# A fused attention and two-expert-layer kernel: the sign step of the weights' conversion as a parametric relu on ScalarE, the low-part subtractions on VectorE

## The chip, the cores and the metric

The kernel runs on one core of a Trainium2 chip. The metric is the time of the whole program in device microseconds (us), lower is better. The core's engines work side by side, each through its own queue in order: TensorE (PE, matmuls), VectorE (DVE), ScalarE (ACT), GpSimd (POOL) and SyncE (SP, which issues the transfers).

## The reference

The reference chains three layers over 2304 tokens (4 batches of 576):

```python
attn = masked_softmax(q @ k.T / 8) @ v        # 8 heads: 4 with a local mask, 4 with a strided one
x = attn as (2304, 512)
h = x @ w_in                                  # 512 -> 2048
g = np.maximum(h, 0.0) ** 2
x = g @ w_out                                 # 2048 -> 512
# soft mixture of experts: 8 experts of 4 slots each
d = softmax(x @ phi, over tokens);  slots = d.T @ x
slot_out = relu(slots[e] @ w1[e]) @ w2[e]
out = softmax(x @ phi, over slots) @ slot_out
```

`w_in` and `w_out` arrive as float64 (the inputs' scaling makes them so), and the kernel is handed their raw 64-bit patterns as pairs of 32-bit words.

## The kernel before, in words

**Stages.** The tokens go in six blocks of 384. In the first stage ("the head") the attention of the first batch and part of the second is computed, the weights of the middle layer are converted, and the first block's products of that layer start as soon as their weights are there. From then on the products of blocks 1 to 5 follow, with the rest of the attention and the dispatch of the soft mixture between them; at the end come the experts and the combination.

**Products.** For each of 16 chunks `f` of the 2048 hidden columns, `gemm1` makes `h` from 12 matmuls (line 409 of the listing, weights in a high and a low part times the tokens `xr` in a high and a low part), `square` on ScalarE makes `r` (line 416) and its square's high part `gh` (419) and the full square (421), `square_low` the low part `gl` (425, VectorE or GpSimd by the letters in `LOW`), and `product` adds three groups of matmuls into `acc_ps` (434 with `gh`, 431 with `gl`).

**Conversion.** The weights go by 16 pairs of chunks `m`, each chunk a 128 x 512 tile that is loaded as 128 x 1024 words (`raw`). Four generators make one pair:

- `split1` (ScalarE): the high words, read as float32 and scaled by 2^-112, into `y` (line 362).
- `split2`: the sign step. Where `MIN[m]` is D, one `scalar_tensor_tensor` on VectorE over the pair, 128 x 1024 (line 376: times 2^32, then the smaller of that and `y`, so that negative values get another scale). Where it is P (pairs 0 and 13), two more relus on ScalarE (370) and two additions on GpSimd (373). Then, on VectorE, a shift of the bits by 3 (line 378, 128 x 1024) and, for each chunk, a merge with the low word's top bits (382, 128 x 512).
- `split3` (ScalarE): the cast of `y` to the high part of `w` (line 389).
- `split4` (GpSimd): the low part of `w`, `y` minus the high part (line 396, 128 x 512).

`y` alternates between two tiles, so pair `m + 2` may only be written when the low part of pair `m` is made.

**What sets the order.** The head's order is a string, `HEAD`: each word is a step (W for `split1` then `split2`, X for `split3`, Y for `split4`, S, C, E, T, V for the attention, R, L, g, H, O for the products, l, q, v for loads), and each word advances its generator to the next `yield`. A word for a generator that has ended does nothing:

```python
                next(parts[step], None)
```

So each engine's queue holds the head's instructions in the order of the string. From the second block on the orders of PE and SP are written out, and the others are placed by priority.

Of the kernel before, what the change touches and what calls it, by code (L numbers as in the profile page):

```python
# [33 lines left out]
LOW = 'DPDPPDDDPPPDDDPP'  # L34
MIN = 'PDDDDDDDDDDDDPDD'
WARM = 6
# [23 lines left out]
def body(tc, qd, kd, vl, vs, win, wout, phi, w1, w2, cst, out):  # L60
# [3 lines left out]
    with ExitStack() as base, ExitStack() as order:  # L64
# [20 lines left out]

# [1 line left out]
        c = cp.tile([128, C_END], F32, name="c")  # L87
# [13 lines left out]

# [1 line left out]
        class Buf:  # L103
            """Queries, keys (block-diagonal over the two heads, 32 zeros ahead), values; scores and weights."""

# [54 lines left out]
        def heads(k, a, n):  # L160
            """Columns a.. a+n of both heads' keys."""
            v = k[:, a:a + n]
            return bass.AP(v.tensor, v.offset, [v.ap[0], (S, 2), (1, n)])

        class Unit:
            """One batch and head pair: queries x keys, softmax, transposed, times values."""

            def __init__(self, b, p, u, qk_tags=("at", "at"), engines="PP", part="AB"):
                """A local unit may come in two parts: of an odd batch, A has the tokens of the first block that it is in."""
                self.b, self.p, self.u, self.part = b, p, u, part  # L170
                self.local = p < 2
                if self.local:
                    self.th = slice(0 if "A" in part else 2, 10 if "B" in part else 4)
                self.view = u.sl[:, self.th] if self.local else u.ss
                n = self.view.shape[1]
                self.mx = tiny[:, 1 if self.local else 3, 0:n]
                self.su = tiny[:, 0 if self.local else 2, 0:n]
                self.qk_tags = qk_tags
                self.ce, self.ne = (DVE if e == "D" else POOL for e in engines)
                self.nm = f"{b}_{p}"  # L180
# [67 lines left out]
            def transpose_pe(self, engines, tags=None):  # L248
                """The same through the tensor engine; each copy out by the engine that its letter names (D in `moves_dve`)."""
                o = wide.rearrange("p a b -> p (a b)")  # L250
# [38 lines left out]
            def values(self):  # L289
                p, u = self.p, self.u  # L290
                # the batch's tokens by the ring's thirds: third, its column, first token, tokens
                segs = [(1, T // 2, 0, T // 2), (2, 0, T // 2, T)] if self.b % 2 else [(0, 0, 0, T), (1, 0, T, T // 2)]
# [42 lines left out]

# [1 line left out]
        # A float64's high word read as a float32 has its exponent in steps of 8; times 2^-112  # L337
        # the exponent field becomes float32's own (2^-80 for negatives: the sign moves to the
        # bit that the shift by 3 takes to the top). The low word gives the last 3 bits.
        # The chunks go by order of first use, two at a time, each to its slot of the weights' space;  # L340
        # slots not yet filled hold the incoming bits and the values on their way.
        NW = 2 * NF
# [11 lines left out]
        def split1(m):  # L354
            if m == NF - 1:
                y = ys[m] = bt[:, 4:6]
            else:
                if m < 2:
                    ys["tile", m] = slot(NW - 2 + m, [128, 2, 512], F32, f"y{m}")
                y = ys[m] = ys["tile", m % 2]  # L360
            for z in range(2):
                ACT.activation(y[:, z], raws[2 * m + z][:, :, 1].bitcast(F32), AF.Relu if MIN[m] == "P" else AF.Copy, scale=2.0 ** -112)  # L362
                yield

        def split2(m):
            y = ys[m]
            if MIN[m] == "P":
                hi = [raws[2 * m + z][:, :, 1].bitcast(F32) for z in range(2)]
                for h in hi:
                    ACT.activation(h, h, AF.Relu, scale=-2.0 ** -80)  # L370
                    yield
                for z in range(2):
                    POOL.tensor_tensor(out=y[:, z], in0=hi[z], in1=y[:, z], op=ALU.add)
                    yield
            else:
                DVE.scalar_tensor_tensor(out=y, in0=y, scalar=2.0 ** 32, in1=y, op0=ALU.mult, op1=ALU.min)  # L376
                yield
            DVE.tensor_scalar(y.bitcast(U32), y.bitcast(U32), 3, None, op0=ALU.logical_shift_left)  # L378
            for z in range(2):
                yield  # L380
                yb = y[:, z].bitcast(U32)
                DVE.scalar_tensor_tensor(out=yb, in0=raws[2 * m + z][:, :, 0], scalar=29, in1=yb,  # L382
                                         op0=ALU.logical_shift_right, op1=ALU.bitwise_or)
# [8 lines left out]
        def split4(m):  # L392
            for z in range(2):
                kind, f = W_ORDER[2 * m + z]
                w = (w_in, w_out)[kind][f]
                POOL.tensor_tensor(out=w[:, 1], in0=ys[m][:, z], in1=w[:, 0].bitcast(F32), op=ALU.subtract)  # L396
                yield

# [1 line left out]
        hs, rs, gh, gl = {}, {}, {}, {}  # L400
# [39 lines left out]

# [1 line left out]
        m_run, s_run = st[:, 0:1], st[:, 1:2]  # L442
# [8 lines left out]
        class Dispatch:  # L451
# [17 lines left out]
            def soft(self):  # L469
# [4 lines left out]
                if self.last:  # L474
                    # one maximum for the three groups of tokens
                    for j in range(3):
                        DVE.tensor_tensor(out=st[0:32, 8 + j:9 + j], in0=st[q(j), 2:3], in1=st[q(j), 0:1], op=ALU.max)
                    DVE.tensor_reduce(out=st[0:32, 11:12], in_=st[0:32, 8:11], op=ALU.max, axis=AX.X)
                    for j in range(3):
                        DVE.tensor_scalar_mul(st[q(j), 3:4], st[0:32, 11:12], -1.0)  # L480
                else:
                    DVE.tensor_tensor(out=bm, in0=bm, in1=m, op=ALU.max)
                    DVE.tensor_scalar_mul(nm, bm, -1.0)
# [37 lines left out]

# [1 line left out]
        # In the order of use; a tile goes to the next space that falls free.  # L523
        e_order = [(k, g, j, z) for k in range(2) for g in range(2) for z in range(4) for j in range(4)]
# [19 lines left out]
        def load_e_ring(n):  # L544
            """Three tiles in the ring's n-th third, after its last use."""
            t = ringp.tile([128, 6, 512], F32, tag=f"ring{n}", bufs=1, name=f"ring{n}_{e_next[0]}")
            for y in range(3):
                load_e(lambda name: t[:, 2 * y:2 * y + 2])
# [3 lines left out]

# [1 line left out]
        order.enter_context(tc.manual_schedule())  # L554
# [4 lines left out]
        def keep_warm(n=1, a=ident, b=c[:, 0:256]):  # L559
            """Products that nothing reads: the array's clock falls when it stands still."""  # L560
            for _ in range(n):
# [61 lines left out]

# [1 line left out]
        bg = {}  # L625
# [16 lines left out]
        def last_products(g):  # L642
            """The last two slots', two of the three token groups ahead of the third."""
            for j in range(2):
# [48 lines left out]

# [1 line left out]
        d = Dispatch(NBLK - 1, last=True)  # L695
# [32 lines left out]

# [1 line left out]
        # Transposed, an expert's four slots go to four copies k = 0..3, so that group j's 32 rows of the  # L730
        # second product are (k, group of experts, slot): two copies become the high part, two the low.
        hsb = [bt[:, n] for n in range(2)]
# [4 lines left out]
        def refill(z):  # L737
            """Tiles of the first group's w1, read by now, take what is still to come."""
            for n in range(4 * z, 4 * z + 4):
# [22 lines left out]
        def turn(g, n):  # L762
            ht = acc_ps[2] if n else ps("mo", f"ht{g}")
            for z in range(4):
                # w2's rows lie in pairs, an even and an odd one in each partition
                h_ = hsb[n][:, 256 * (z // 2):256 * (z // 2) + 256].rearrange("p (x a) -> p a x", a=2)[:, z % 2, :]
# [15 lines left out]

# [1 line left out]
        spare = [freed[4 + n] for n in range(16)]  # L784
# [108 lines left out]
```

## Time and profile before

| | |
|---|---|
| three runs | 583.48, 583.71, 584.54 us; median 583.71 us |
| profiled execution, first to last instruction (span) | 583.3 us; no time beside its span is recorded for it |
| PE busy over the span | 547.7 us (94%) |
| VectorE, ScalarE, GpSimd busy over the span | 269.6, 249.7, 103.2 us |
| the same in the stretch from 48 to 121 us: PE, VectorE, ScalarE, GpSimd | 58.47, 69.29, 43.88, 51.10 us of 73 |

Busy time is what an engine spent in its own instructions; a busy share over the whole span averages stages with different limits, so the stretches are read apart. The head ends at about 142 us, when the last pair of weights is converted; 441 of the 583 us lie behind it. The runs lie within 0.2% of each other, so the comparison below calls a change of less than 0.2% no change.

### The profile page before, as it was taken

Reading aid. Unit: us, or ns where it says so; the run is one execution under the profiler, and the core shown is the slowest. Engines: PE = TensorE matmul, PEld = TensorE weight load, DVE = VectorE, ACT = ScalarE, POOL = GpSimd, SP = SyncE. Lnnn points to the kernel's source line nnn. Section 1 sums busy time; section 2 is a strip of 40 time slices with the busy share of each in tenths; the row PEclk is TensorE's granted clock in tenths of the full one; section 3 lists DMA queues with packets and bytes.
Section 4 is the critical chain, followed back from the end, with each engine's and each line's share of the span. In section 5 each row is a group of like instructions: output and inputs, shape, how many; then the busy total and the mean of one; then the engine's idle time right before and its main releaser. Section 6 shows DMA issues by size and latency. Waiting matters only on the chain.

```text
span 583.3 us, 10033 instructions
## 1 busy us (share of the span) xinstructions
PE 547.7 (94%) x4092; PEld 454.4 (78%) x4092; DVE 269.6 (46%) x565; ACT 249.7 (43%) x541; POOL 103.2 (18%) x95
## 2 busy tenths in 40 slices
PE   7878887889999999999999999999999999999994
PEld 5657666767988988888888888898889988984442
DVE  6998999954154316566135574211211113122322
ACT  2476655657443334443344343343433543341232
POOL 4528566734011001010001010000000000001000
PEclk8889999879999999999999999999999999999998
DMA  9976431330010101210221210340002566669946
GB/s 295 345 273 218 176 112 55 117 107 24 0 42 22 44 22 42 78 44 22 78 64 42 69 34 36 128 198 0 1 1 77 191 230 224 240 231 328 402 168 220
DMA packets 27117, 72.87 MB, mean 125 GB/s; under 512 B 3008, under 2 KB 8640, under 8 KB 27072
## 3 DMA queue, kind: packets, MB, share of 16 engines
q1 hardware_dynamic: 27072, 72.24, 35.2%
q8 instruction: 32, 0.52, 0.4%
q14 instruction: 13, 0.11, 0.1%
HBM read 67.51 MB, written 4.72 MB: 124 GB/s over the span
## 4 chain that ended last, share of the span: by engine, by line
PE 77%; DVE 15%; ACT 3%; issue 2%; DMA 1%; POOL 1%; SPq 0%; ACTq 0%; POOLq 0%
PE h L409 30%; PE acc_ps L434 21%; PE acc_ps L431 10%; DVE y L382 3%; PE acc_ps L779 3%; PE eh L755 2%; DVE y L376 2%; DVE y L378 2%; PE oa L311 1%; PE ob L311 1%; PE x2t L458 1%; PE lg L466 1%; DVE ptl L245 1%; DMA bt<-kd 1%; PE qa L191 1%
## 5 line engine op out<-in xcount | busy, mean ns | idle before, releaser
L409 PE MATMUL h<-xr,w 128*128 128x384 f32 x1152 | 224.7, 342 | 4.2 <-ACT r L416 3.0
L409 PEld LDWEIGHTS h<-xr,w 128*128 128x128 f32 x1152 | 207.3, 191 | 15.0 <-ACT r L416 4.8
L434 PE MATMUL acc_ps<-w,gh 128*128 128x512 f32 x576 | 155.1, 403 | 1.1 <-POOL w L396 1.1
L416 ACT ACTIVATE r<-h 128x384 f32<-128x384 f32 x96 | 47.1, 491 | 200.2 <-PE h L409 196.9
L425 DVE TENSOR_TENSOR gl<-r,gh 128x384 fp32r<-128x384 f32 x88 | 53.5, 608 | 169.6 <-ACT r L421 165.6
L434 PEld LDWEIGHTS acc_ps<-w,gh 128*128 128x128 f32 x576 | 104.3, 189 | 26.6 <-ACT gh L419 2.7
L431 PE MATMUL acc_ps<-w,gl 128*128 128x512 f32 x288 | 82.7, 394 | 4.4 <-DVE gl L425 4.4
L431 PEld LDWEIGHTS acc_ps<-w,gl 128*128 128x128 f32 x288 | 53.5, 188 | 17.7 <-DVE gl L425 6.3
L396 POOL TENSOR_TENSOR w<-y,w 128x512 fp32r<-128x512 f32 x30 | 46.0, 1543 | 34.6 <-ACT w L389 33.2
L419 ACT ACTIVATE gh<-r 128x384 fp32r<-128x384 f32 x96 | 50.0, 524 | 2.6
L421 ACT ACTIVATE r<-r 128x384 f32<-128x384 f32 x96 | 50.2, 525 | 2.0
L217 POOL TENSOR_TENSOR sl<-sl,tiny 128x640 f32<-128x640 f32 (+2 forms) x10 | 12.2, 1219 | 144.1 <-DVE tiny L214 144.1
L245 DVE STREAM_TRANSPOSE ptl<-sl 32x320 f32<-32x320 f32 (+2 forms) x72 | 31.3, 435 | 6.8 <-POOL sl L232 5.3
L735 POOL MEMSET bt<- 128x512 f32 x4 | 2.0, 525 | 175.8 <-PE lg L466 172.5
L389 ACT CAST w<-y 128x512 fp32r<-128x512 f32 x30 | 18.4, 618 | 18.4 <-DVE y L382 18.3
L382 DVE SCALAR_TENSOR_TENSOR y<-raw,y 128x512 uint32<-128x512 uint32 x26 | 25.2, 977 | 0.3
L362 ACT ACTIVATE y<-raw 128x512 f32<-128x512 f32 x26 | 17.3, 677 | 10.3 <-DMA raw<-win 10.3
L562 PE MATMUL warm<-el 128*128 128x256 f32 x54 | 19.0, 514 | 1.1 <-POOL el L555 1.1
L376 DVE SCALAR_TENSOR_TENSOR y<-y 128x1024 f32<-128x1024 f32 x13 | 19.3, 1488 | 0.8 <-ACT y L362 0.8
L562 PEld LDWEIGHTS warm<-el 128*128 128x128 f32 x54 | 13.6, 265 | 4.1 <-POOL el L555 1.1
L200 DVE SCALAR_TENSOR_TENSOR sl<-qa,c 128x128 f32<-128x128 f32 (+3 forms) x18 | 6.3, 375 | 20.7 <-PE qa L191 15.7
L245 DVE STREAM_TRANSPOSE pts<-sw 32x512 f32<-32x512 f32 x20 | 14.1, 703 | 3.7 <-POOL sw L232 3.4
(173 smaller groups left out, 481.1 us busy)
## 6 DMA issues: line engine op xcount, KB each, us to landing
e<-w SPq DMA_DIRECT2D x49, 512.0 KB, 4.6
ring<-w SPq DMA_DIRECT2D x15, 512.0 KB, 9.1
raw<-win SPq DMA_DIRECT2D x14, 512.0 KB, 6.2
raw<-wout SPq DMA_DIRECT2D x12, 512.0 KB, 8.4
out<-ob SPq DMA_DIRECT2D x18, 256.0 KB, 2.8
q<-qd SPq DMA_DIRECT2D x15, 288.0 KB, 3.6
k<-kd SPq DMA_DIRECT2D x30, 144.0 KB, 3.7
v<-vs SPq DMA_DIRECT2D x7, 512.0 KB, 4.2
```

Of the source, the lines that this page charges most:

```text
L245: DVE.transpose(out=dst, in_=src)
L376: DVE.scalar_tensor_tensor(out=y, in0=y, scalar=2.0 ** 32, in1=y, op0=ALU.mult, op1=ALU.min)
L382: DVE.scalar_tensor_tensor(out=yb, in0=raws[2 * m + z][:, :, 0], scalar=29, in1=yb, op0=ALU.logical_shift_right, op1=ALU.bitwise_or)
L396: POOL.tensor_tensor(out=w[:, 1], in0=ys[m][:, z], in1=w[:, 0].bitcast(F32), op=ALU.subtract)
L409: PE.matmul(hs[g][0][:, 0:T], w_in[f][:, a, 128 * kc:128 * kc + 128], xr[i % 3][:, x, kc, :], start=hs[g][1] == 0, stop=hs[g][1] == 11)
L416: ACT.activation(r, h[:, 0:T], AF.Relu)
L419: ACT.activation(gh[g], r, AF.Square)
L421: ACT.activation(r, r, AF.Square)
L425: (POOL if LOW[g:g + 1] == "P" else DVE).tensor_tensor(out=gl[g], in0=rs.pop(g), in1=gh[g].bitcast(F32), op=ALU.subtract)
L431: PE.matmul(a, gl[g][:, 128 * j:128 * j + 128], w[:, 0], start=False, stop=f == NF - 1)
L434: PE.matmul(a, gh[g][:, 128 * j:128 * j + 128], w[:, z], start=f == 0 and z == 0, stop=False)
L562: PE.matmul(warm[:, 0:256], a, b, start=True, stop=True)
```

## The change

The sign step moves into `split1`: a parametric relu on ScalarE (scale 2^-112, slope 2^32 for negative values) writes `y` as the sign step left it. `split2` starts with the shift; its VectorE instruction for 14 pairs and the two relus and two additions for each of the other 2 pairs are gone. The low-part subtraction of `split4` goes to VectorE for all 16 pairs. Comments and docstrings are also dropped, so the same code stands some ten lines higher afterwards (378 becomes 368, 382 becomes 372, 396 becomes 386, 425 becomes 415).

```diff
-MIN = 'PDDDDDDDDDDDDPDD'
+SUB = 'DDDDDDDDDDDDDDDD'
...
             for z in range(2):
-                ACT.activation(y[:, z], raws[2 * m + z][:, :, 1].bitcast(F32), AF.Relu if MIN[m] == "P" else AF.Copy, scale=2.0 ** -112)
+                ACT.activation(y[:, z], raws[2 * m + z][:, :, 1].bitcast(F32), AF.Prelu, scale=2.0 ** -112, alpha=2.0 ** 32)
                 yield
 
         def split2(m):
             y = ys[m]
-            if MIN[m] == "P":
-                hi = [raws[2 * m + z][:, :, 1].bitcast(F32) for z in range(2)]
-                for h in hi:
-                    ACT.activation(h, h, AF.Relu, scale=-2.0 ** -80)
-                    yield
-                for z in range(2):
-                    POOL.tensor_tensor(out=y[:, z], in0=hi[z], in1=y[:, z], op=ALU.add)
-                    yield
-            else:
-                DVE.scalar_tensor_tensor(out=y, in0=y, scalar=2.0 ** 32, in1=y, op0=ALU.mult, op1=ALU.min)
-                yield
             DVE.tensor_scalar(y.bitcast(U32), y.bitcast(U32), 3, None, op0=ALU.logical_shift_left)
...
-                POOL.tensor_tensor(out=w[:, 1], in0=ys[m][:, z], in1=w[:, 0].bitcast(F32), op=ALU.subtract)
+                (POOL if SUB[m] == "P" else DVE).tensor_tensor(out=w[:, 1], in0=ys[m][:, z], in1=w[:, 0].bitcast(F32), op=ALU.subtract)
```

The string `HEAD` is the same. Since `split2` has one `yield` less for 14 pairs and four less for two, the shift and the merges of a pair stand one word earlier in it (four earlier for pairs 0 and 13), and the last words of each W do nothing. The orders on PE and SP are the same, row for row.

VectorE's queue in the middle of the head, from the scaled scores `ss` of a strided unit to the low part `gl` of the first hidden chunk and the next pair's first step. Before (`y_214` and `y_234` are the two tiles of `y`, `tiny` the softmax's maxima and sums):

```order
L210 SCALAR_TENSOR_TENSOR ss_97<-qa_2_554,c 128x288
L214 TENSOR_REDUCE tiny<-ss_97 128x16
L376 SCALAR_TENSOR_TENSOR y_214<-y_214 128x1024
L378 TENSOR_SCALAR y_214<-y_214 128x1024
L382 SCALAR_TENSOR_TENSOR y_214<-raw_301,y_214 128x512
L224 TENSOR_REDUCE tiny<-ss_97 128x16
L382 SCALAR_TENSOR_TENSOR y_214<-raw_453,y_214 128x512
L226 TENSOR_SCALAR tiny<-tiny 128x16
L227 RECIPROCAL tiny<-tiny 128x16
L229 TENSOR_SCALAR tiny<-tiny,c 128x16
L425 TENSOR_TENSOR gl_685<-r_619,gh_631 128x384
L376 SCALAR_TENSOR_TENSOR y_234<-y_234 128x1024
```

The same place on VectorE with the change:

```order
L210 SCALAR_TENSOR_TENSOR ss_97<-qa_2_547,c 128x288
L386 TENSOR_TENSOR w_580<-y_234,w_580 128x512
L214 TENSOR_REDUCE tiny<-ss_97 128x16
L368 TENSOR_SCALAR y_214<-y_214 128x1024
L372 SCALAR_TENSOR_TENSOR y_214<-raw_299,y_214 128x512
L372 SCALAR_TENSOR_TENSOR y_214<-raw_448,y_214 128x512
L224 TENSOR_REDUCE tiny<-ss_97 128x16
L386 TENSOR_TENSOR w_657<-y_214,w_657 128x512
L226 TENSOR_SCALAR tiny<-tiny 128x16
L227 RECIPROCAL tiny<-tiny 128x16
L229 TENSOR_SCALAR tiny<-tiny,c 128x16
L415 TENSOR_TENSOR gl_677<-r_612,gh_624 128x384
```

The two instructions of line 376 are gone from the stretch, and two subtractions (line 386) stand in it, one of the pair before (`w_580`) and one of this pair (`w_657`), the latter ahead of the sums and of `gl`.

GpSimd's queue at the same place of the program, before:

```order
L396 TENSOR_TENSOR w_587<-y_234,w_587 128x512
L217 TENSOR_TENSOR ss_97<-ss_97,tiny 128x288
L425 TENSOR_TENSOR gl_661<-r_624,gh_637 128x384
L396 TENSOR_TENSOR w_664<-y_214,w_664 128x512
L232 TENSOR_TENSOR sw_98<-ss_97,tiny 128x16x18
L396 TENSOR_TENSOR w_683<-y_214,w_683 128x512
L396 TENSOR_TENSOR w_731<-y_234,w_731 128x512
L396 TENSOR_TENSOR w_748<-y_234,w_748 128x512
L425 TENSOR_TENSOR gl_782<-r_754,gh_765 128x384
```

And with the change:

```order
L217 TENSOR_TENSOR ss_97<-ss_97,tiny 128x288
L415 TENSOR_TENSOR gl_654<-r_617,gh_630 128x384
L232 TENSOR_TENSOR sw_98<-ss_97,tiny 128x16x18
L415 TENSOR_TENSOR gl_772<-r_745,gh_756 128x384
```

What stays on GpSimd are the attention's subtractions and products with the softmax's values (217, 232) and the `gl` of the chunks that `LOW` gives it.

## Rows read from the trace of the kernel before

**Rows 1.** Page: busy time of each engine, share of the span, instructions.

```profile
PE 547.7 (94%) x4092; PEld 454.4 (78%) x4092; DVE 269.6 (46%) x565; ACT 249.7 (43%) x541; POOL 103.2 (18%) x95
```

**Rows 2.** Busy time by stretch, with granted clock (PEclk) and share of transfers.

```profile
0.00:48.00 48.00, 37.74 (x472) 29.64 (x472) 39.38 (x73) 24.40 (x56) 22.48 (x28) 0.86 0.83 279
48.00:121.00 73.00, 58.47 (x381) 47.53 (x379) 69.29 (x96) 43.88 (x89) 51.10 (x38) 0.96 0.40 141
121.00:142.00 21.00, 19.86 (x116) 16.88 (x115) 10.50 (x15) 14.10 (x39) 7.84 (x7) 0.89 0.20 67
142.00:583.00 441.00, 431.66 (x3132) 360.35 (x3130) 150.48 (x382) 167.36 (x358) 21.74 (x24) 1.00 0.31 108
```

**Rows 3.** Chain of waits from 48 to 121 us, shares by engine and line.

```profile
by line: DVE y L382 22.8%; DVE y L376 19.2%; DVE y L378 13.6%; issue 12.6%; DVE gl L425 6.0%; DVE ptl L245 4.1%; DVE tiny L226 4.0%; DVE pts L245 3.0%; ACT y L362 2.6%; DVE tiny L224 1.9%; DVE xr L330 1.5%; PE oa L311 1.5%; DVE sl L200 1.2%
```

**Rows 4.** Who PE waited for, 48 to 142 us: total, times, longest.

```profile
PE acc_ps L431 <- DVE gl L425: 4.4, 4, 1.6
PE oa L311 <- issue: 3.5, 2, 1.8
PE h L409 <- ACT r L416: 3.0, 3, 1.3
PE ob L311 <- DVE sl L200: 2.2, 1, 2.2
```

**Rows 5.** The longest of PE's waits from 142 us to the end.

```profile
PE out L815 <- DVE s L808: 1.0, 1, 1.0
```

**Rows 6.** VectorE's instructions by line, 48 to 121 us: busy, mean ns.

```profile
L382 DVE SCALAR_TENSOR_TENSOR y<-raw,y 128x512 uint32<-128x512 uint32 x18 | 19.9, 1111 | 0.3
L376 DVE SCALAR_TENSOR_TENSOR y<-y 128x1024 f32<-128x1024 f32 x9 | 14.5, 1606 | 0.3 <-ACT y L362 0.2
L378 DVE TENSOR_SCALAR y<-y 128x1024 uint32<-128x1024 uint32 x10 | 11.4, 1147 | 0.1
L425 DVE TENSOR_TENSOR gl<-r,gh 128x384 fp32r<-128x384 f32 x6 | 5.2, 870 | 0.0
L226 DVE TENSOR_SCALAR tiny<-tiny 128x16 f32<-128x16 f32 (+1 forms) x4 | 3.1, 774 | 0.0
```

**Rows 7.** VectorE's instructions by line and shape, 9 to 48 us.

```profile
L376 DVE SCALAR_TENSOR_TENSOR y<-y 128x1024 f32<-128x1024 f32 x3 | 3.7, 1223 | 0.0
```

**Rows 8.** GpSimd in order of time: start, duration, idle before.

```profile
31.88 1.50 POOL L396 TENSOR_TENSOR w<-y,w 128x512 fp32r<-128x512 f32 x1
43.87 6.17 POOL L396 TENSOR_TENSOR w<-y,w 128x512 fp32r<-128x512 f32 x4 [10.49 <-ACT w L389]
...
62.14 1.49 POOL L396 TENSOR_TENSOR w<-y,w 128x512 fp32r<-128x512 f32 x1 [2.81 <-ACT w L389]
```

**Rows 9.** VectorE in order of time, at those places and two others.

```profile
33.38 0.17 DVE L226 TENSOR_SCALAR tiny<-tiny 128x16 f32<-128x16 f32 x1
...
41.32 0.68 DVE L382 SCALAR_TENSOR_TENSOR y<-raw,y 128x512 uint32<-128x512 uint32 x1
41.92 0.68 DVE L378 TENSOR_SCALAR y<-y 128x1024 uint32<-128x1024 uint32 x1
...
62.39 1.78 DVE L382 SCALAR_TENSOR_TENSOR y<-raw,y 128x512 uint32<-128x512 uint32 x1
...
95.60 0.54 DVE L425 TENSOR_TENSOR gl<-r,gh 128x384 fp32r<-128x384 f32 x1
```

**Rows 10.** GpSimd's instructions by line, 48 to 121 us.

```profile
L396 POOL TENSOR_TENSOR w<-y,w 128x512 fp32r<-128x512 f32 x22 | 34.2, 1566 | 12.5 <-ACT w L389 11.1 <-DMA raw<-win 1.3
...
L373 POOL TENSOR_TENSOR y<-bt,y 128x512 f32<-128x512 f32 x2 | 2.6, 1307 | 0.4 <-ACT bt L370 0.4
```

**Rows 11.** Who GpSimd waited for most, 9 to 142 us: total, times, longest.

```profile
POOL w L396 <- ACT w L389: 34.5, 14, 10.5
```

**Rows 12.** ScalarE's conversion instructions by line, 48 to 121 us.

```profile
L389 ACT CAST w<-y 128x512 fp32r<-128x512 f32 x20 | 12.2, 617 | 18.3 <-DVE y L382 18.3
L362 ACT ACTIVATE y<-raw 128x512 f32<-128x512 f32 x18 | 12.0, 676 | 0.2 <-DMA raw<-win 0.2
```

**Rows 13.** Busy time and granted clock, 121 to 128 us, columns as in rows 2.

```profile
121.00:128.00 7.00, 7.00 (x32) 6.37 (x31) 4.12 (x6) 2.31 (x7) 0.47 (x1) 0.66 0.37 119
```

## The prediction

> **What bounds the kernel now.** I read the page's busy times first. PE is busy 94% of the span [rows 1], so only time in which PE stands can be won, and the question is where it stands. The table by stretch answers that: from 142 us to the end PE is busy 431.66 of 441 us at the full granted clock, but before that only 37.74 of 48, 58.47 of 73 and 19.86 of 21 us [rows 2]. The change touches only the head, whose last conversion ends at about 142 us; the orders on PE and SP are the same. Behind 142 us the longest thing that PE waits for is 1.0 us, at the very end [rows 5], so what the head gains or loses arrives at the end nearly one for one.
>
> In the middle stretch, 48 to 121 us, VectorE is busy 69.29 of 73 us [rows 2], and the chain of waits runs along it: its three conversion lines alone hold 22.8, 19.2 and 13.6% of the chain, 56% of 73 us [rows 3]. PE's waits name the same engine: 4.4 us for `gl`, 2.2 us for VectorE directly, 3.0 us for ScalarE's `r` [rows 4], and ScalarE itself stood 18.3 us at its casts until VectorE's merge was done [rows 12]. So from 48 to 121 us VectorE is the bound, and 73 - 58.47 = 14.5 us is the most that PE can win there by standing less. From 0 to 48 us the transfers take 0.83 of their engines' time [rows 2], so VectorE is one limit of several. From 121 to 142 us it is busy half the time.
>
> **A second thing that the reader should see.** VectorE's durations are not constant. A merge (line 382) takes 0.68 us and a shift (378) 0.68 us at 41 to 42 us [rows 9], when GpSimd stands still (its wait of 10.49 us ends at 43.87) [rows 8]. In 48 to 121 us, with GpSimd busy 51.10 of 73 us [rows 2], they take 1.111 and 1.147 us on average [rows 6]. One merge that starts at 62.39 lasts 1.78 us; a GpSimd subtraction stands from 62.14 to 63.63 [rows 8, 9]. From 62.39 to 63.63 are 1.24 us, and 0.68 more make 1.92: the merge takes nearly as long as if it had waited for GpSimd to end. The small instruction of line 226 takes 0.17 us at 33.38, when GpSimd stands [rows 8, 9], and 0.774 on average in the stretch [rows 6].
>
> **The change, part by part**, in the stretch 48 to 121 us first.
>
> *Removed from VectorE:* nine sign steps, 14.5 us [rows 6].
>
> *Shorter on VectorE, because GpSimd is mostly empty:* the excess of what stays over its quiet duration is 18 x (1.111 - 0.68) = 7.8 for the merges, 10 x (1.147 - 0.68) = 4.7 for the shifts, 6 x (0.870 - 0.54) = 2.0 for `gl`, 4 x (0.774 - 0.17) = 2.4 for line 226 [rows 6, 9], together 16.9 us. GpSimd loses its subtractions and additions, 34.2 + 2.6 = 36.8 [rows 10] of 51.10 us [rows 2], 72%. I take the excess to fall by that share: 12.2 us. Bounds: 0, if GpSimd is not the reason; 2.6, if everything that stays on GpSimd, 51.1 - 36.8 = 14.3 us, still holds VectorE up in full; and 16.9.
>
> *Added to VectorE:* 22 subtractions [rows 10]. The trace has none on VectorE. The nearest below is `gl`, the same operation on 384 columns, quiet 0.54 us; the nearest above a merge with GpSimd in the way, 1.111 us; the merge has the same 512 columns and two inputs, so I take its quiet 0.68 us [rows 6, 9] plus 28% of its excess, 0.12: 0.80 us, 17.6 us in all (11.9 to 24.4).
>
> *A rule against this.* The row shows a merge that outlasts a GpSimd instruction by its own quiet time. The Trainium skill (SBUF — State Buffer, "Who interferes with whom") says that a VectorE instruction with two SBUF inputs contends with a GpSimd one that reads SBUF, that the port pair is an exclusive lock, and that the loser waits for the whole instruction. The merge at 62.39 agrees. By that rule a two-input subtraction on VectorE is itself open to such waits, and at the worst the lower bound above holds: the excess falls by 2.6 us and 22 x 0.68 = 15.0 us are added, -2.1 us before the added waits in place of the -9.1 that the shares give.
>
> *Waits that the change adds.* A subtraction needs its chunk's cast on ScalarE; GpSimd bore that so far, 34.5 us in 14 waits [rows 11], of which 10.49 stand before 43.87 us [rows 8] and beside the head's other work. On VectorE such a wait holds what is queued behind. In the order shown above, `w_657` stands ahead of the sums, of `gl` and of the next shift, and PE waits for `gl` already, up to 1.6 us [rows 4]. Against that, a subtraction is mostly two or more instructions behind its merge, and a cast takes 0.617 us [rows 12]. I put 1.3 us on the path, from nothing to 12.5, the idle time ahead of GpSimd's 22 subtractions [rows 10].
>
> *Sum for 48 to 121 us:* -14.5 - 12.2 + 17.6 + 1.3 = -7.8 us (-9.1 before the added waits). PE's 14.5 us of standing cover it.
>
> *Before 48 us:* three sign steps, 3.7 us [rows 7], go, eight subtractions come; four of them stand by a moment at 44 to 48 us at which PE is busy with its first products, so I count 4 x 0.68 = 2.7: -1.0 us.
>
> *From 121 to 142 us:* PE's granted clock is 0.66 from 121 to 128 us [rows 13], between its levels of 1.2 and 2.4 GHz, after PE has stood for VectorE and its followers, and 1.00 behind 142 us [rows 2]. If those gaps shrink, up to 7 x (1 - 0.66) = 2.4 us come back. I take them: -2.4.
>
> *ScalarE:* the parametric relu takes the place of a copy on the same 128 x 512 tile, 0.676 us. Below it stands the cast, 0.617; above, twice 0.676, if it took two passes: 18 x 0.676 = 12.2 us on an engine that is busy 43.88 of 73 and stands 18.3 us at casts [rows 2, 12], so even that would mostly be hidden. I take 0.676. The order holds the same single table load as before. If VectorE no longer held ScalarE up, this cover would be gone, and the second pass would cost up to its 12.2 us; I give that little weight.
>
> *GpSimd and SP:* GpSimd's fewer instructions cost nothing. SP's loads of `raw` wait for slots that VectorE frees, and the transfers take 0.40 of their time from 48 us on [rows 2], so they come earlier with it.
>
> **Total:** -7.8 - 1.0 - 2.4 = -11.2 us. Against the profiled 583.3 us that is 572.1; the median of the runs lies 0.4 us above that span, which gives **572.5 us**.
>
> **The rivals.**
>
> *VectorE runs clear and PE becomes the bound (12%).* If all of the excess goes (16.9), a subtraction costs 0.68 (15.0) and no wait is added, the stretch gives -16.4, which PE's 14.5 us cap; with the 1.0 and 2.4 that is -17.9, 565.8 us. For it: GpSimd's rest can fall beside transposes and reductions, whose durations hardly enter the excess. Against: 14.3 us of two-input work stay on GpSimd.
>
> *The subtractions wait for their casts (22%).* VectorE takes its queue in order, and ScalarE's casts stand behind `r`, which stands behind PE (3.0 us of PE's own waits are for `r` [rows 4]). If 6 of the 12.5 us come onto VectorE, -11.2 becomes about -6.5: 577 us. For it: GpSimd's waits show how early these subtractions stand in the string, and `HEAD` is as it was. Against: VectorE comes to them later than an idle GpSimd did.
>
> *Slower (8%): the long durations are VectorE's own.* If merges and shifts stay at 1.111 and 1.147 us and a subtraction costs a merge's 1.111, the stretch gives -14.5 + 24.4 = +9.9 us; with the first stretch at -1.0 the end is +8.9, about 592.6 us. It decides from where a subtraction costs over 14.5 / 22 = 0.66 us and nothing else gets shorter. Against it stand the quiet rows at 41 to 42 us, when VectorE itself was just as busy.
>
> *No change (3%):* everything left on GpSimd holds VectorE up in full, -14.5 - 2.6 + 15.0 = -2.1, and the subtractions wait 5 us for casts: +2.9 in the stretch, -0.5 in all, 583.2 us. For it: the merge at 62.39. Against: 14.3 us of GpSimd would have to meet open instructions every time, and now some 16.9 us are shared out over 51.
>
> **How the numbers follow.** The forecast, -8 to -15 us with the waits and the clock about as taken, gets the remaining 55%, and its own range is 568 to 576 us. The range for 8 in 10 takes all of it, about three quarters of the cast waits (to 579) and most of the PE-bound case (from 565). A measurement here tells about 0.2% (1.2 us) from no change. Faster: 55 + 12 + 22 less the part of the wait case that ends near nothing, 88%; same 4%; slower 8%.
>
> **What would show it.** In the changed kernel's profile: shifts and merges at about 0.7 to 0.8 us on average in the middle of the head, and GpSimd busy some 15 us there; subtractions on VectorE of 0.7 to 0.85 us; the parametric relu at 0.65 to 0.70 us; VectorE waiting for the casts for under 3 us; PE standing some 8 us less before the head's end; the granted clock near 1 in PE's last 20 us of it; and everything behind the head as long as before, 441 us. The prediction is wrong if the shifts and merges stay above 1 us, if VectorE waits for casts in sum above 10 us, or if PE's gaps return at another place, at `r` or at a late `raw` tile.

## The result, and the profile after

The changed kernel takes 565.47 us (median of 4 runs, 564.01 to 566.97) against 584.12 us for the kernel before beside it: ratio 0.968, 95% interval 0.966 to 0.970, 18.7 us or 3.2% faster. Below, a run that is far slower than the others of its kernel (1052.79 us, one of ten of the subtractions alone, and 603.18 us, one of four of the old places) is left out of the median and the ratio. The result is inside the range and on the forecast's side, but 7 us below the forecast of 572.5, and almost exactly where the second case (VectorE runs clear, PE becomes the bound) put it, 565.8 us.

The page's first part, which answers to [rows 1]:

```profile
PE 538.6 (96%) x4092; PEld 449.0 (80%) x4092; DVE 253.0 (45%) x583; ACT 247.0 (44%) x537; POOL 49.1 (9%) x59
```

VectorE has 18 instructions more (32 subtractions in, 14 sign steps out) and 16.6 us less busy time; GpSimd's busy time is halved. To see where the 20 us of the span went I look for the same two places in PE's order: the eight matmuls into `oa` of the last local unit of the head, and the first `h` of 12 matmuls without a break, from which PE runs through. In the timeline of PE before (start, duration, instruction, idle time in front):

```profile
120.08 1.21 PE L311 MATMUL oa<-ptl,v 128*64 128x160 f32 x8 [1.76 <-issue]
...
141.62 2.25 PE L409 MATMUL h<-xr,w 128*128 128x384 f32 x12
```

and after (the second row is cut at the window's end):

```profile
103.92 0.75 PE L311 MATMUL oa<-ptl,v 128*64 128x160 f32 x8 [0.58 <-issue]
...
121.49 1.75 PE L399 MATMUL h<-xr,w 128*128 128x384 f32 x9
```

The first place comes 16.2 us earlier, the second 20.1. The tables by stretch, columns as in [rows 2], cut at these places, before:

```profile
0.00:48.00 48.00, 37.74 (x472) 29.64 (x472) 39.38 (x73) 24.40 (x56) 22.48 (x28) 0.86 0.83 279
48.00:121.20 73.20, 58.67 (x381) 47.64 (x379) 69.29 (x96) 43.88 (x89) 51.30 (x38) 0.96 0.40 141
121.20:141.60 20.40, 19.26 (x111) 16.39 (x110) 10.15 (x15) 14.10 (x39) 7.42 (x7) 0.89 0.21 69
141.60:583.00 441.40, 432.06 (x3134) 360.73 (x3132) 150.82 (x383) 167.36 (x358) 21.97 (x25) 1.00 0.30 108
```

and after:

```profile
0.00:48.00 48.00, 34.95 (x471) 27.32 (x471) 38.41 (x76) 22.70 (x54) 9.13 (x19) 0.93 0.82 279
48.00:104.80 56.80, 55.31 (x392) 46.54 (x383) 54.03 (x109) 43.01 (x88) 15.84 (x14) 1.00 0.52 181
104.80:121.50 16.70, 16.45 (x110) 14.35 (x110) 9.34 (x16) 13.99 (x39) 1.87 (x2) 1.00 0.27 84
121.50:563.00 441.50, 431.94 (x3134) 360.81 (x3132) 151.26 (x384) 167.29 (x359) 22.23 (x25) 1.00 0.31 108
```

Nothing is won before 48 us. The middle goes from 73.2 to 56.8 us, the head's end from 20.4 to 16.7, and the rest is as long as it was. In the middle VectorE's busy time falls from 69.29 to 54.03 us, PE stands 1.5 us where it stood 14.5, and its granted clock is 1.00 instead of 0.96 (and 1.00 instead of 0.89 in the head's end). PE's waits from 40 to 142 us, answering to [rows 4], are nearly gone:

```profile
PE oa L311 <- issue: 0.6, 1, 0.6
PE oa L311 <- PE h L399: 0.4, 1, 0.4
PE acc_ps L421 <- DVE gl L415: 0.3, 1, 0.3
PE ob L311 <- ACT pts L282: 0.2, 1, 0.2
```

The chain of waits in the middle, answering to [rows 3], is led by PE's lines now, and the merges' share is 7.8% instead of 22.8%:

```profile
by line: PE h L399 23.1%; PE acc_ps L424 15.0%; PE acc_ps L421 8.2%; DVE y L372 7.8%; DVE w L386 5.8%; issue 5.8%; DVE pts L245 4.8%; POOL gl L415 4.0%; PE oa L311 3.8%; DVE gl L415 3.4%; DVE ptl L245 2.9%; DVE y L368 2.5%; ACT r L406 2.4%;
```

VectorE's lines there, answering to [rows 6], from 48 to 104.8 us:

```profile
L386 DVE TENSOR_TENSOR w<-y,w 128x512 fp32r<-128x512 f32 x22 | 16.2, 738 | 1.0 <-ACT w L379 0.8
L372 DVE SCALAR_TENSOR_TENSOR y<-raw,y 128x512 uint32<-128x512 uint32 x18 | 12.8, 722 | 0.2
L368 DVE TENSOR_SCALAR y<-y 128x1024 uint32<-128x1024 uint32 x10 | 8.1, 811 | 0.9 <-ACT y L363 0.8
...
L415 DVE TENSOR_TENSOR gl<-r,gh 128x384 fp32r<-128x384 f32 x6 | 3.7, 620 | 0.0
...
L226 DVE TENSOR_SCALAR tiny<-tiny 128x16 f32<-128x16 f32 (+1 forms) x4 | 0.7, 164 | 0.0
```

The reader should see the same 18 merges at 0.722 us that took 1.111, and the 22 subtractions at 0.738 us with 0.8 us of waiting for casts in all. The parametric relu costs what the copy cost (0.672 against 0.676 us):

```profile
L363 ACT ACTIVATE y<-raw 128x512 f32<-128x512 f32 x18 | 12.0, 672 | 1.6 <-DMA raw<-win 1.2 <-DMA raw<-wout 0.4
```

### The profile page after: what moved, and what is told of

Read it like the earlier page. It is cut to its first block, busy times and chain, and to the rows that moved or that the text cites. A ratio compares the mean times of both kernels' runs of the same rounds, so it can differ in the third digit from the quotient of the medians.

```text
span 563.1 us, 9991 instructions
## 1 busy us (share of the span) xinstructions
PE 538.6 (96%) x4092; PEld 449.0 (80%) x4092; DVE 253.0 (45%) x583; ACT 247.0 (44%) x537; POOL 49.1 (9%) x59
## 4 chain that ended last, share of the span: by engine, by line
PE 85%; DVE 5%; ACT 4%; DMA 3%; issue 1%; POOL 1%; ACTq 0%; POOLq 0%
PE h L399 33%; PE acc_ps L424 23%; PE acc_ps L421 11%; PE acc_ps L769 3%; PE eh L745 3%; PE ob L311 2%; PE oa L311 2%; DMA raw<-win 2%; PE x2t L448 1%; PE lg L456 1%; PE qa L191 1%; PE out L805 1%; DVE w L386 1%; PE sa L494 1%; DMA k<-kd 1%
## 5 line engine op out<-in xcount | busy, mean ns | idle before, releaser
L399 PE MATMUL h<-xr,w 128*128 128x384 f32 x1152 | 220.4, 338 | 0.2
L399 PEld LDWEIGHTS h<-xr,w 128*128 128x128 f32 x1152 | 204.1, 188 | 9.9 <-ACT r L406 1.0
L415 DVE TENSOR_TENSOR gl<-r,gh 128x384 fp32r<-128x384 f32 x88 | 51.6, 586 | 164.7 <-ACT r L411 157.4
L386 DVE TENSOR_TENSOR w<-y,w 128x512 fp32r<-128x512 f32 x30 | 21.7, 725 | 5.1 <-ACT w L379 4.9
L372 DVE SCALAR_TENSOR_TENSOR y<-raw,y 128x512 uint32<-128x512 uint32 x26 | 18.2, 710 | 0.3
L552 PE MATMUL warm<-el 128*128 128x256 f32 x54 | 16.8, 464 | 1.1 <-POOL el L545 1.1
L769 PE MATMUL acc_ps<-e,bt 128*32 128x256 f32 x184 | 15.5, 384 | 0.0
L200 DVE SCALAR_TENSOR_TENSOR sl<-qa,c 128x128 f32<-128x128 f32 (+3 forms) x18 | 6.3, 375 | 20.4 <-PE qa L191 15.3
L552 PEld LDWEIGHTS warm<-el 128*128 128x128 f32 x54 | 12.1, 235 | 3.6 <-POOL el L545 1.1
```

What stands on the lines that cost most here:

```text
L386: (POOL if SUB[m] == "P" else DVE).tensor_tensor(out=w[:, 1], in0=ys[m][:, z], in1=w[:, 0].bitcast(F32), op=ALU.subtract)
L399: PE.matmul(hs[g][0][:, 0:T], w_in[f][:, a, 128 * kc:128 * kc + 128], xr[i % 3][:, x, kc, :], start=hs[g][1] == 0, stop=hs[g][1] == 11)
L415: (POOL if LOW[g:g + 1] == "P" else DVE).tensor_tensor(out=gl[g], in0=rs.pop(g), in1=gh[g].bitcast(F32), op=ALU.subtract)
L552: PE.matmul(warm[:, 0:256], a, b, start=True, stop=True)
L769: PE.matmul(so[n][q(j), 0:256], hT[g][fc // 4][:, fc % 4, q(j)], cols(ex[1, g, j, fc // 2], 512 * (fc % 2) + 256 * n, 256), start=g == 0 a ...
```

## The experiments

Two theories at the start. **A:** GpSimd's subtractions lengthen whatever VectorE does beside them, so putting them on VectorE costs about what it gives back there, and the sign step's removal is the rest. **B:** VectorE's durations have nothing to do with GpSimd; the gain is the sign step, or the order, or that nothing waits for GpSimd's low parts any more. The table sums up the runs; "from first `h` to unbroken `h`" is read from PE's timeline in the profile of each, from the start of the head's first 12 matmuls into `h` to the place found above. It leaves out scatter in the stage before; the first column of starts shows how large that is. The last column scatters too: in the two profiles of the changed kernel it differs by 1.9 us.

| kernel | median us | ratio to before, interval | first `h` | unbroken `h` | between |
|---|---|---|---|---|---|
| before | 584.12 | 1 | 42.42 | 141.62 | 99.2 |
| changed | 565.47 | 0.968 (0.966 to 0.970) | 43.17 | 121.49 | 78.3 |
| changed, again | 565.1 | 0.967 (0.964 to 0.970) | 44.41 | 124.60 | 80.2 |
| sign step alone | 568.7 | 0.974 (0.970 to 0.977) | 41.54 | 125.09 | 83.6 |
| subtractions alone | 579.85 | 0.992 (0.990 to 0.995) | 45.83 | 138.86 | 93.0 |
| changed, old places | 566.42 | 0.969 (0.965 to 0.973) | 42.98 | 123.58 | 80.6 |
| changed, GpSimd reads beside | 579.35 | 0.992 (0.989 to 0.994) | 45.38 | 134.04 | 88.7 |
| changed, GpSimd writes beside | 570.14 | 0.976 (0.972 to 0.980) | 42.37 | 124.73 | 82.4 |
| changed, no subtractions | 562.64 | 0.962 (0.959 to 0.966) | 40.60 | 116.61 | 76.0 |

**The sign step alone.** The changed kernel with

```diff
-SUB = 'DDDDDDDDDDDDDDDD'
+SUB = 'PPPPPPPPPPPPPPPP'
```

> The changed kernel with all low-part subtractions on GpSimd again; the sign step stays in ScalarE's parametric relu. Theory (GpSimd's subtractions lengthen what VectorE does beside them): VectorE has 14.5 us less to do between 48 and 121 us, but merges and shifts stay at 1.0 to 1.15 us, so part of the gain is there, 9 to 13 us: 571 to 575 us. Rival (the sign step alone is the gain, the subtractions' place does not matter): the changed kernel's time, 565 us, with a margin of 2.

Measured: 568.7 us, 15.5 us below the 584.21 us of before beside it, between the two expectations: more than the 9 to 13 us of theory A. The sign step's removal is most of the gain; the 3.2 us left to the changed kernel are 0.6%, and the ratios' intervals just touch, so I take from it that the other half of the change gives some 3 us beside it, not a precise figure. VectorE's durations from 48 to 115 us:

```profile
L372 DVE SCALAR_TENSOR_TENSOR y<-raw,y 128x512 uint32<-128x512 uint32 x18 | 15.8, 889 | 0.3
L368 DVE TENSOR_SCALAR y<-y 128x1024 uint32<-128x1024 uint32 x11 | 12.4, 1128 | 3.0 <-ACT y L363 2.9
```

With GpSimd's subtractions in place the shifts stay at 1.128 us, as theory A says. The merges, at 0.889, are longer than the changed kernel's 0.722 but miss the 1.0 to 1.15 that I had written: 0.22 of their fall from 1.111 came with the sign step's removal alone. Why is not shown.

**The subtractions alone.** The kernel before with

```diff
-                POOL.tensor_tensor(out=w[:, 1], in0=ys[m][:, z], in1=w[:, 0].bitcast(F32), op=ALU.subtract)
+                DVE.tensor_tensor(out=w[:, 1], in0=ys[m][:, z], in1=w[:, 0].bitcast(F32), op=ALU.subtract)
```

> The kernel before with the low-part subtractions on VectorE; the sign step stays where it was. Theory: VectorE takes 22 subtractions of about 0.74 us (16 us) in the stretch and gives back the excess of its merges, shifts, low parts and sign steps, some 17 us (the sign steps fall from 1.6 to about 1.25 us); about nothing is left, 580 to 587 us, with merges at about 0.72 us. Rival (durations have nothing to do with GpSimd): 16 us more on the bounding engine, 595 us or more, with merges at 1.1 us.

Measured: 579.85 us, 4.4 us faster than before, 0.15 us below theory A's 580 to 587; the rival, 595 us or more, is out. VectorE has 32 instructions more and is no later: between the first `h` and the eight matmuls into `oa`, before and then in this run (columns as in [rows 2]), it is busy 3.3 us less.

```profile
42.42:120.08 77.66, 63.13 (x484) 52.01 (x483) 72.89 (x104) 48.38 (x100) 54.31 (x39) 0.96 0.39 135
45.83:117.78 71.95, 62.40 (x486) 51.20 (x483) 69.58 (x126) 48.77 (x100) 18.20 (x16) 0.97 0.43 145
```

Its lines from 48 to 115 us:

```profile
L382 DVE SCALAR_TENSOR_TENSOR y<-raw,y 128x512 uint32<-128x512 uint32 x20 | 14.9, 752 | 0.2
L396 DVE TENSOR_TENSOR w<-y,w 128x512 fp32r<-128x512 f32 x20 | 13.8, 688 | 0.1
L376 DVE SCALAR_TENSOR_TENSOR y<-y 128x1024 f32<-128x1024 f32 x9 | 11.9, 1317 | 0.1
```

The sign steps that took 1.606 us [rows 6] take 1.317, the merges 0.752 instead of 1.111. The two halves add up: 15.5 + 4.4 = 19.9 us against 18.7 for both.

**Shifts and merges at their old places.** The changed kernel with empty steps where the sign step was:

```diff
             y = ys[m]
+            for _ in range(4 if m in (0, 13) else 1):
+                yield
             DVE.tensor_scalar(y.bitcast(U32), y.bitcast(U32), 3, None, op0=ALU.logical_shift_left)
```

> The changed kernel with empty steps in place of the sign step, so that shifts and merges stand in the queues where they stood before (one word later, four for pairs 0 and 13). Theory (durations make the gain, not places): the changed kernel's time within 1.5 us, 564 to 567 us. Rival (the earlier place of the shift is part of the gain): 568 us or more.

Measured: 566.42 us, ratio 0.969 against 0.968: no difference that these runs can tell. The profile has 80.6 us between the two places, where the changed kernel's two profiles have 78.3 and 80.2. The earlier places are no large part of the gain.

**GpSimd's reads put back.** The changed kernel, with a load on GpSimd beside each subtraction that nobody waits for:

```diff
+        idle = cp.tile([128, 256], F32R, name="idle")
...
                 (POOL if SUB[m] == "P" else DVE).tensor_tensor(out=w[:, 1], in0=ys[m][:, z], in1=w[:, 0].bitcast(F32), op=ALU.subtract)
+                for n in range(2):
+                    v = w[:, 0, 256 * n:256 * n + 256].bitcast(F32)
+                    POOL.tensor_tensor(out=idle, in0=v, in1=v, op=ALU.subtract)
```

> The changed kernel, and beside each subtraction on VectorE GpSimd subtracts the same chunk's high part from itself into a scratch tile that nothing reads, in two halves of 128 x 256: the load on GpSimd of before, with nothing waiting for its result. Theory (VectorE is held up by what GpSimd reads beside it): merges and subtractions go from 0.72 to 1.0 us or more, and the time rises by 6 to 14 us, 571 to 580 us. Rival (the gain came from dependences: nothing has to wait for GpSimd's low parts any more): durations and time stay, 565 to 567 us. A second rival (GpSimd's full queue makes its other work late): the time rises, but VectorE's durations stay at 0.7 us.

Measured: 579.35 us, 13.9 us slower than the changed kernel. VectorE's lines from 48 to 115 us:

```profile
L387 DVE TENSOR_TENSOR w<-y,w 128x512 fp32r<-128x512 f32 x21 | 19.3, 920 | 1.4 <-ACT w L380 1.3
L373 DVE SCALAR_TENSOR_TENSOR y<-raw,y 128x512 uint32<-128x512 uint32 x19 | 17.0, 907 | 0.2
L369 DVE TENSOR_SCALAR y<-y 128x1024 uint32<-128x1024 uint32 x10 | 8.8, 882 | 0.1
```

Subtractions go from 0.738 to 0.920 us, merges from 0.722 to 0.907, short of the 1.0 that I had written but clearly up; gone dependences cannot explain it, since nothing reads the scratch tile. PE's longest waits (48 to 140 us) are for `gl` from VectorE, not for GpSimd:

```profile
PE acc_ps L425 <- DVE gl L419: 5.7, 4, 1.8
```

**GpSimd's load without the reads.** The same with

```diff
+                v = w[:, 0, 0:16].bitcast(F32)
+                POOL.tensor_tensor(out=idle[:, 0:16], in0=v, in1=v, op=ALU.subtract)
+                for n in range(4):
+                    POOL.memset(idle.bitcast(F32), 0.0)
```

> The same, but GpSimd only writes: a subtraction of 16 columns, which waits for the cast, and four memsets of 128 x 256 into the scratch tile. Theory (what holds up an instruction with two inputs is GpSimd's reading): merges and subtractions stay at 0.7 to 0.75 us, shifts may be longer; the time rises by less than 3 us, 565 to 568 us. Rival (any GpSimd work, or its queue, does it): durations and time as in the run with the reads, 571 us or more.

Measured: 570.14 us, 4.7 us slower than the changed kernel and 9 us faster than with the reads. GpSimd is as busy as in the run before it, 88 memsets and 23 small subtractions from 48 to 115 us:

```profile
L391 POOL MEMSET idle<- 128x256 f32 x88 | 29.8, 339 | 5.1
L389 POOL TENSOR_TENSOR idle<-w 128x16 fp32r<-128x16 f32 x23 | 9.8, 428 | 6.6 <-ACT w L380 5.6
```

and VectorE's durations beside it are

```profile
L387 DVE TENSOR_TENSOR w<-y,w 128x512 fp32r<-128x512 f32 x22 | 15.0, 687 | 4.8 <-ACT w L380 4.7
L373 DVE SCALAR_TENSOR_TENSOR y<-raw,y 128x512 uint32<-128x512 uint32 x18 | 12.4, 704 | 0.2
L369 DVE TENSOR_SCALAR y<-y 128x1024 uint32<-128x1024 uint32 x11 | 9.6, 871 | 0.6 <-ACT y L364 0.5
```

The instructions with two inputs are at their quiet duration, so it is GpSimd's reading that holds them up. The shifts' mean of 0.871 us is no measure of the writes: three of the eleven began while GpSimd made a `gl`, from two inputs, and took 1.18 to 1.51 us, while four that began inside a memset took 0.68 or 0.69. The longest and the instruction beside it:

```profile
70.35 1.51 DVE L369 TENSOR_SCALAR y<-y 128x1024 uint32<-128x1024 uint32 x1
69.89 1.42 POOL L420 TENSOR_TENSOR gl<-r,gh 128x384 fp32r<-128x384 f32 x1
```

The 4.7 us are more than the 3 that I gave it. PE's waits (48 to 140 us) are for `gl`, with 0.8 us for a GpSimd result that came late, so part of it is GpSimd's queue; how much, these runs do not split:

```profile
PE acc_ps L426 <- DVE gl L420: 2.0, 2, 1.6
PE oa L312 <- issue: 1.3, 1, 1.3
PE pt L258 <- POOL sw L233: 0.8, 1, 0.8
```

**No subtractions at all.** The changed kernel with

```diff
-                (POOL if SUB[m] == "P" else DVE).tensor_tensor(out=w[:, 1], in0=ys[m][:, z], in1=w[:, 0].bitcast(F32), op=ALU.subtract)
+                POOL.memset(w[:, 1].bitcast(F32), 1e-4)
```

> The changed kernel without its low-part subtractions: GpSimd writes a constant over each low part instead, so the low parts of the weights are left out of the result. VectorE has about 16 us less to do between 48 and 105 us. Theory (PE, busy 97% there, has become the bound): the head ends at most some 2.5 us earlier, 563 to 565.5 us. Rival (VectorE, busy 95% there, is still the bound): 10 us or more, 556 us or less.

Measured: 562.64 us, 2.5 us below the 565.1 of the changed kernel measured beside it, though VectorE had some 16 us less to do. That is 0.4 us below the theory's range, the intervals of the two ratios overlap, and the rival, 556 us or less, is out. In the same stretch as above PE does not stand at all:

```profile
48.00:104.80 56.80, 56.80 (x400) 49.31 (x399) 47.41 (x88) 42.98 (x91) 23.69 (x36) 1.00 0.53 181
```

So PE is the bound there after the change, and the 16.2 us of subtractions cost some 2.5 us of time where they now stand.

**Some subtractions on GpSimd again.** Of the first two pairs (`SUB = 'PPDDDDDDDDDDDDDD'`), then also of the last two (`'PPDDDDDDDDDDDDPP'`).

> The changed kernel with the subtractions of the first two pairs on GpSimd, which stands still for most of the time before 48 us. Theory (before 48 us VectorE's queue is one limit, and its chain holds two of these subtractions, 0.6 us each): 0.5 to 1.5 us faster, 564 to 565 us. Rival (transfers and PE's own chain set that part): no difference, or slower by what GpSimd's reads hold up, 565.5 to 567 us.

Measured: 563.74 us, ratio 0.965 (0.962 to 0.968), 1.7 us below the changed kernel, but its profile has PE at the same places as the changed kernel's first: the last two times eight matmuls into `oa` start at 92.47 and 103.92 us in both. I ran it again with the changed kernel itself:

> The changed kernel as it is, on this chip, beside the next two: 564 to 567 us.

> The subtractions of the first two pairs on GpSimd once more. If the 1.7 us seen before are this edit's, the time lies 1 us or more below the changed kernel's of the same call; if they are scatter (the profiles agree at 92 and 104 us), within 0.7 us of it.

> The subtractions of the first two and of the last two pairs on GpSimd. At the head's end VectorE waits for casts and PE is the bound, and a subtraction on GpSimd takes 1.3 us against 0.7: no gain at that end, 0 to 1 us slower than with the first two alone. Rival (VectorE's waits there delay low parts): 1 us faster.

Measured together: 565.1 us for the changed kernel (ratio 0.967, 0.964 to 0.970), 564.53 for the first two pairs (0.966, 0.963 to 0.969), 564.56 for first and last two (0.966, 0.964 to 0.969). The 1.7 us were scatter for the most part; no version here is shown to beat the changed kernel.

## Why the prediction was right, and where its sizes were off

**The mechanism** came as forecast: shifts and merges at 0.811 and 0.722 us, subtractions at 0.738, 0.8 us of waits for casts, everything behind the head as long as before. The size did not: 18.7 us where 11.2 were forecast. The range holds the result by half a microsecond, because its lower end was set for a case with a chance of 12%.

**The bound** was read rightly: VectorE from 48 to 121 us, nothing behind 142 us. PE's 14.5 us of standing were taken as the most that the middle could give; 13.0 of them came back, and the middle gave 16.4, because PE's busy time fell as well.

**The sign steps, -14.5 us in the middle:** right in size; alone they gave 15.5 us in time, with somewhat shorter merges in it. The 3.7 us before 48 us gave nothing that shows (the first `h` starts at 43.17 instead of 42.42, within the scatter of the table), so no run shows the -1.0.

**The excess that falls away, -12.2 us,** was too small: "I take the excess to fall by that share", 72%. Merges give 18 x (1.111 - 0.722) = 7.0, shifts 10 x (1.147 - 0.811) = 3.4, `gl` 6 x (0.870 - 0.620) = 1.5 us, 11.9 of their 14.5, or 82%. Before, 10 of the 18 merges took over 1 us; in the changed kernel it is 2 of 18, fewer than the 28% of GpSimd's work that stayed would give, and 3 of the 10 shifts and 2 of the 22 subtractions. All seven began while a GpSimd instruction with two inputs was running. One of them, and what ran beside it:

```profile
85.81 1.17 DVE L368 TENSOR_SCALAR y<-y 128x1024 uint32<-128x1024 uint32 x1
84.97 1.46 POOL L415 TENSOR_TENSOR gl<-r,gh 128x384 fp32r<-128x384 f32 x1 [10.31 <-DVE sl L200]
```

Why so few of them meet is not shown.

**The added subtractions, 17.6 us,** were 22 x 0.738 = 16.2: the merge's quiet duration plus 0.06 in place of 0.12. **The added waits, 1.3 us,** were 0.8 in the stretch. At the place named for it the wait is 0.33 us (VectorE's timeline after: `w_657` behind the sums' first step, then `gl`):

```profile
52.49 0.44 DVE L224 TENSOR_REDUCE tiny<-ss 128x16 f32<-128x288 f32 x1
53.26 0.73 DVE L386 TENSOR_TENSOR w<-y,w 128x512 fp32r<-128x512 f32 x1 [0.33 <-ACT w L379]
...
54.55 0.55 DVE L415 TENSOR_TENSOR gl<-r,gh 128x384 fp32r<-128x384 f32 x1
```

`gl` starts at 54.55 us, where it started at 56.00 before. With 2.4 us of line 226 (0.774 to 0.164 us) and 0.8 of line 229 (0.650 to 0.234), the corrected sum is -14.5 - (11.9 + 2.4 + 0.8) + 16.2 + 0.8 = -12.6 us in place of -7.8. VectorE's busy time fell by 15.3 us, 1.9 more than these parts without the waits; that stays open. Moving the subtractions, which the sum had at -12.2 + 17.6 + 1.3 = +6.7, comes to +1.9 by these sizes, about nothing. In the run of that half alone the sign steps, still there, get shorter as well, by 9 x (1.606 - 1.317) = 2.6 us, and it gains 4.4 us.

**The clock, -2.4 us from 121 us on,** was a term too narrow: the granted clock went from 0.96 to 1.00 in the middle too. PE's account by the tables above shows the whole. Of the middle's 16.4 us, 13.0 are standing (14.5 to 1.5) and 3.4 are PE's busy time (58.67 to 55.31); of the 3.7 us of the head's end, 0.9 are standing (1.14 to 0.25) and 2.8 busy time (19.26 to 16.45). The clock's own rise, 0.04 of 73.2 us and 0.11 of 20.4 us, makes 2.9 and 2.2 of that busy time. That smaller gaps bring the clock back, as the prediction had it, is not shown. In the run with the reads PE stands 10.1 us between 48 and 116.46 us, in gaps of up to 1.8 us, and keeps the full clock there and behind; the subtractions alone, with 9.6 us of standing, have 0.97 and then 0.85:

```profile
48.00:116.46 68.46, 58.39 (x474) 48.13 (x472) 65.77 (x112) 45.13 (x93) 53.48 (x59) 1.00 0.44 152
117.78:138.86 21.08, 20.60 (x117) 17.14 (x118) 13.35 (x19) 13.89 (x39) 1.79 (x3) 0.85 0.21 66
```

**The total** was set 0.4 us above the span, from the median of three runs and the span of another execution. In the changed kernel's four runs the time lies 1.7 to 1.8 us above the span of the same execution. By the two profiled spans the gain is 20.2 us, by the medians 18.7.

**The rivals.** PE as the new bound, with 12%, was the case that came, at 565.8 us; the run without subtractions shows PE without a gap. That 565.8 lies 0.3 us from the measured time is in part luck: it is made of 14.5 us in the middle, 1.0 before it and 2.4 behind, where the profiles have 16.4, nothing and 3.7. Casts that hold VectorE up did not come where VectorE was the bound. That the long durations are VectorE's own is out by the run with the reads and the one with the writes. **The rule of the Trainium skill** (SBUF — State Buffer, "Who interferes with whom") agrees with those two runs: two-input instructions are at 0.907 and 0.920 us beside GpSimd's reads, at 0.704 and 0.687 beside its writes. By it the subtractions on VectorE were open to such waits; only 2 of 22 took over 1 us in the middle, since the same change took most of GpSimd's work away.

## What to carry to other kernels

Before moving work off GpSimd onto a full VectorE, compare the durations of VectorE's instructions beside GpSimd's work and without it: here what stayed on VectorE got some 15 us shorter, against 16.2 us of subtractions that moved there. When two engines are near the bound, price the freed engine's gain up to the next bound, and look at PE's granted clock apart: here PE's busy time fell by some 6 us with it, beside the standing. A step on the bounding engine that another engine's existing instruction can take in may cost nothing there (here 0.672 us against 0.676), so look for functions that do both.

## What the runs showed of the hardware that was not expected

What counted between VectorE and GpSimd was which of the two began first. Before, a merge that began at 52.24 us, ahead of a GpSimd instruction at 52.63, kept its quiet 0.69 us, where the one at 62.39 [rows 9] began behind and took 1.78:

```profile
52.24 0.69 DVE L382 SCALAR_TENSOR_TENSOR y<-raw,y 128x512 uint32<-128x512 uint32 x1
52.63 1.19 POOL L425 TENSOR_TENSOR gl<-r,gh 128x384 fp32r<-128x384 f32 x1 [0.97 <-ACT r L421]
```

A merge with two inputs was held up by GpSimd's reads and not by its memsets (0.907 us against 0.704). A shift with one input (128 x 1024, 0.69 us quiet) was held up by memsets too: in the run without subtractions, where four of 128 x 512 follow each other without a gap, one took 1.38 us.

```profile
71.08 1.38 DVE L368 TENSOR_SCALAR y<-y 128x1024 uint32<-128x1024 uint32 x1
69.99 1.93 POOL L386 MEMSET w<- 128x512 f32 x4
```

PE's granted clock in the head's last part went from 0.89 to 1.00 with the change. Gaps of one to two microseconds ahead of it went too, but the run with the reads had such gaps and kept 1.00, so what brought the clock back is open.
